# Loading K and V for two batches at a time in a decode attention kernel

## The chip, the cores and the metric

The kernel runs on one core of a Trainium2 chip. The time is that of the device, in microseconds (us), from the start to the end of one execution; the median of three runs of the kernel before is 202.74 us (202.69 to 202.88). The profile is of one further execution of 202.94 us. A core has a TensorE for matmuls (PE; its weight loads are PEld), a VectorE (DVE), a ScalarE (ACT), a GpSimd (POOL), a SyncE that issues most transfers (SP), and 16 DMA engines that move the data between device memory and the on-chip memories' 128 partitions. TensorE's results go to PSUM, everything else lies in SBUF.

## The reference

There are two branches on the same input `x` (8 batches, one token, 448 features), mixed by a sigmoid gate `g`. Branch A is attention over a cache; branch B is a layer norm and a small MLP.

```python
W = min(4096, max(256, Sk // 4))           # Sk = 4096, so W = 1024 keys
q = (x @ wq) -> [B=8, Hq=16, 1, Dh=256]
k = k_cache[:, :, Sk - W:, :]              # [8, Hkv=8, 1024, 256], each used by rep = 2 heads
v = v_cache[:, :, Sk - W:, :]
p = softmax(q k^T * Dh ** -0.5)            # over the 1024 keys
a = (p v) -> [8, 4096] @ wo                # wo: 4096 x 448
b = gelu(layernorm(x) @ w1 + b1) @ w2 + b2
return g * a + (1 - g) * b                 # all tensors bfloat16
```

Only the last 1024 of 4096 keys of each cache are read: 8 batches x 8 KV heads x 1024 keys x 256 features x 2 bytes is 32 MB for K and as much for V.

## The kernel before, in words

**Setting.** A *pair* `n` is one KV head `g` and one batch `b` (`g, b = divmod(n, 8)`), 64 pairs in all; the eight pairs of one head are a *group*. A tile of K or of V is one pair: 128 partitions with `NC = 8` keys of 256 features each, so that partition p holds the keys 8p to 8p + 7, 4 KB that are contiguous in device memory. The whole tile is 512 KB in one piece.

**Loads.** `load` (L116 to L119) takes a tile from `kvpool`, which has `NKV = 23` buffers, and issues one transfer on SP. The order of issue is the list `units` (L137 to L145): K of pair 0, 1, 2, ...; from pair 11 on a V tile after each K tile, eleven pairs behind (`NB + LAG`, 8 + 3); after each eighth K the 448 KB of `wo` that this group needs; at the end the last eleven V tiles and the last piece of `wo`. Ahead of them SP issues `x`, `w1`, `w2`, three transfers of `wq` with 8 KB per partition (L134), and the rest of `wq`, `wq_t` (L135). There are eight DMA semaphores in turn, so each transfer of SP waits for the landing of the one eight places before it; from the 24th tile on it also waits until TensorE has read the tile whose buffer it takes.

**TensorE's order.** Nothing reorders the program: the schedule is written by hand (`manual_schedule`), and each engine works through its instructions in the order of the text. First come the MLP (`mlp_up`, `mlp_down`) and the q projection. Then a loop of 75 steps `n` (L428 to L455) does, in each step,

- `transposes(n)`: 16 transposes of 128 x 128 turn the K tile round into PSUM, and two copies on VectorE bring it to SBUF as `kt` (L314, L319);
- `scores(n - 1)`: 16 matmuls with `kt` as weights and the two query heads of this batch as 2 columns (L330). The scores of a group stand in one PSUM bank `G[g]`: keys on the partitions, and 8 chunks x 16 columns (8 batches x 2 heads) beside each other;
- in the first three steps of the next group the softmax of the last one: `soft_max1` takes the maximum over chunks on VectorE, `soft_max2` a transpose and the maximum over the partitions, and splits it in three bfloat16 parts; `soft_exp` subtracts it by a matmul into the scores and applies the exponential on ScalarE (L370, L377), 128 columns in each;
- `pv(n - 11)`: 16 matmuls with the V tile as weights and 2 columns of the exponentials (L396), summing over the chunks;
- after the last `pv` of a group `soft_sum`: 8 matmuls with a matrix of ones sum the exponentials (L382), VectorE takes the reciprocal and scales (`o_scale`, L387, L407); one step later `o_proj` multiplies by `wo` into `A_ps` (L421).

After the loop the last `o_proj`, the mix with branch B (L458) and the store follow.

Of the kernel before, what the change touches and what calls it, by code (L numbers as in the profile page):

```python
# [9 lines left out]
ALU = mybir.AluOpType  # L10
AXIS = mybir.AxisListType
BF16 = mybir.dt.bfloat16
# [4 lines left out]
def kernel(  # L17
# [15 lines left out]
    nc = tc.nc  # L33
    P = nc.NUM_PARTITIONS

    B, Sq, D = A_x.shape
    _, Hkv, Sk, Dh = A_k_cache.shape
    HD = A_wq.shape[1]
    Hq = HD // Dh
    rep = Hq // Hkv  # L40
    W = min(4096, max(256, Sk // 4))
    kv0 = Sk - W
    F = B_w1.shape[1]
    NB = B
    NJ = Dh // P
    NC = W // P
    NF = F // P
    R = NB * rep
    DC = D // P
    DM = DC * P  # L50
    TL = D - DM
    HH = HD // 2
    assert Sq == 1 and Dh % P == 0 and W % P == 0 and F % P == 0
    assert TL * 2 == P and TL % 32 == 0 and NC * R <= P and 3 * 32 <= P and R <= 32
    qscale = float(Dh) ** -0.5
    NPAIR = NB * Hkv
    LAG = 3
    NKV = 23


    S0 = 0
    O0 = S0 + NC * R
    Z0 = O0 + NJ * R
    T0 = Z0 + R

# [3 lines left out]
    consts = ctx.enter_context(tc.tile_pool(name="consts", bufs=1))  # L69
    kvpool = ctx.enter_context(tc.tile_pool(name="kvpool", bufs=NKV))  # L70
    ktpool = ctx.enter_context(tc.tile_pool(name="ktpool", bufs=3))
# [15 lines left out]
    gw_sb = consts.tile([NB, D], BF16, name="gw_sb")  # L87
    wq_sb = consts.tile([P, DC, HD], BF16, name="wq_sb")
    wq_t = consts.tile([P, HH], BF16, name="wq_t")
    w1_sb = consts.tile([P, DC, F], BF16, name="w1_sb")  # L90
    w1_t = consts.tile([P, F], BF16, name="w1_t")
# [4 lines left out]
    ident = consts.tile([P, P], BF16, name="ident")  # L96
    identf = consts.tile([P, P], F32, name="identf")
    onesb = consts.tile([P, P], BF16, name="onesb")
    diag = [consts.tile([P, R], BF16, name=f"diag{k}") for k in range(2)]
    qT = consts.tile([P, NJ, Hkv, NB, rep], BF16, name="qT")  # L100
    xT = consts.tile([P, DC + 2, NB], BF16, name="xT")
    yT = consts.tile([P, DC + 1, NB], BF16, name="yT")
    x_e = consts.tile([NB, 2, P], BF16, name="x_e")
# [3 lines left out]
    res = consts.tile([NB, D], BF16, name="res")  # L107


    def k_src(src, n):  # L110
        g, b = divmod(n, NB)
        return src[b, g, kv0:Sk, :].rearrange("(p c) d -> p c d", c=NC)

    KV = {}

    def load(kind, n):  # L116
        t = kvpool.tile([P, NC, Dh], BF16, tag="kv", name="kv")
        nc.sync.dma_start(t[:], k_src(A_k_cache if kind == "K" else A_v_cache, n))  # L118
        KV[kind, n] = t  # L119

    nc.sync.dma_start(x_sb[:], xf)
# [3 lines left out]
    nc.sync.dma_start(  # L125
        w1_sb[:], B_w1[0:DM, :].rearrange("(p c) n -> p c n", c=DC)
    )
# [6 lines left out]
        nc.sync.dma_start(wq_sb[:, c, :], wq_v[:, c, :])  # L134
    nc.sync.dma_start(wq_t[:], A_wq[DM:D, :].rearrange("r (h n) -> (r h) n", h=2))  # L135

    units = []  # L137
    for n in range(NPAIR):
        units.append(("K", n))
        if n % NB == NB - 1 and n // NB < Hkv - 1:  # L140
            units.append(("W", n // NB))
        if n - NB - LAG >= 0:
            units.append(("V", n - NB - LAG))
    units += [("V", m) for m in range(NPAIR - NB - LAG, NPAIR)]
    units += [("W", Hkv - 1)]  # L145
    pos = [0, 0]

    def issue_to(k):
        while pos[0] < len(units):
            kind, n = units[pos[0]]  # L150
            if kind == "W":
                r0 = n * NKH * P
                nc.sync.dma_start(
                    wo_sb[n][:],
                    A_wo[r0 : r0 + NKH * P, :].rearrange("(k p) n -> p k n", p=P),
                )
            else:
                if pos[1] == k:
                    return
                load(kind, n)  # L160
                pos[1] += 1
            pos[0] += 1

    issue_to(NKV)


    make_identity(nc, ident[:])
    nc.gpsimd.memset(onesb[:], 1.0)
    for t in diag:
        nc.gpsimd.memset(t[:], 0.0)  # L170
    nc.gpsimd.memset(x_e[:], 0.0)
# [108 lines left out]
    for c in range(DC + 1):  # L280
        for k in range(NQ):
            if c < DC:
                w, xs = wq_sb[:, c, k * P : (k + 1) * P], xT[:, c, :]
            else:
                h, kk = divmod(k, NQ // 2)
                w, xs = wq_t[:, kk * P : (kk + 1) * P], xT[:, DC + h, :]
            nc.tensor.matmul(
                q_ps[:, k * NB : (k + 1) * NB],
                lhsT=w,
                rhs=xs,  # L290
                start=(c == 0 and k == 0),
                stop=(c == DC),
                skip_group_check=True,
# [9 lines left out]
    G = {}  # L303
    E = {}
# [1 line left out]
    RZ = {}  # L306

    def transposes(n):
        K = KV.pop(("K", n))
        kt = ktpool.tile([P, NJ, W], BF16, tag="kt", name="kt")  # L310
        for j in range(NJ):
            ktp = ps_kt.tile([P, W], BF16, tag="ktp", name="ktp")
            for c in range(NC):
                nc.tensor.transpose(  # L314
                    ktp[:, c * P : (c + 1) * P],
                    K[:, c, j * P : (j + 1) * P],
                    ident[:],
                )
            nc.vector.tensor_copy(kt[:, j, :], ktp[:])  # L319
        KT[n] = kt  # L320

    def scores(n):
        g, b = divmod(n, NB)
        kt = KT.pop(n)
        if b == 0:
            G[g] = ps_g.tile([P, 512], F32, tag="grp", name="grp")
        for c in range(NC):
            for j in range(NJ):
                s = S0 + c * R + b * rep
                nc.tensor.matmul(  # L330
                    G[g][:, s : s + rep],
                    lhsT=kt[:, j, c * P : (c + 1) * P],
                    rhs=qT[:, j, g, b, :],
                    start=(b == 0 and c == 0 and j == 0),
                    stop=(j == NJ - 1),
                    skip_group_check=True,
                )
# [42 lines left out]
    def soft_sum(g):  # L380
        for c in range(NC):
            nc.tensor.matmul(  # L382
                G[g][:, Z0 : Z0 + R], lhsT=onesb[:], rhs=E[g][:, c * R : (c + 1) * R],
                start=False, stop=(c == NC - 1), skip_group_check=True,
            )
        rz = work.tile([P, R], F32, tag="rz", name="rz")
        nc.vector.reciprocal(rz[:], G[g][:, Z0 : Z0 + R])  # L387
        RZ[g] = rz

    def pv(m):  # L390
        g, b = divmod(m, NB)
        V = KV.pop(("V", m))
        for j in range(NJ):
            for c in range(NC):
                o = O0 + j * R + b * rep
                nc.tensor.matmul(  # L396
                    G[g][:, o : o + rep],
                    lhsT=V[:, c, j * P : (j + 1) * P],
                    rhs=E[g][:, c * R + b * rep : c * R + (b + 1) * rep],
                    start=False,  # L400
                    stop=(c == NC - 1),
                    skip_group_check=True,
                )

    def o_scale(g):
        ot = work.tile([P, NJ, R], BF16, tag="ot", name="ot")
        nc.vector.tensor_tensor(  # L407
            ot[:],
            G[g][:, O0 : O0 + NJ * R].rearrange("p (j r) -> p j r", j=NJ),
            RZ[g][:].unsqueeze(1).to_broadcast([P, NJ, R]),  # L410
            op=ALU.mult,
        )
        OT[g] = ot

    def o_proj(g):
        ot = OT[g]
        for i in range(rep):
            for j in range(NJ):
                k = i * NJ + j
                w = wo_sb[g][:, k, :]  # L420
                nc.tensor.matmul(  # L421
                    A_ps[:],
                    lhsT=ot[:].rearrange("p j (b i) -> p j i b", i=rep)[:, j, i, :],
                    rhs=w,
                    start=(g == 0 and k == 0),
                    stop=(g == Hkv - 1 and k == NKH - 1),
                )


    LAST = NPAIR + NB + LAG  # L430
    done = 0
    for n in range(LAST):
        if n < NPAIR:
            transposes(n)
            done += 1
        if 0 <= n - 1 < NPAIR:
            scores(n - 1)
        g, r = divmod(n, NB)
        if g >= 1 and g - 1 < Hkv:
            if r == 0:  # L440
                soft_max1(g - 1)
            if r == 1:
                soft_max2(g - 1)
            if r == 2:
                soft_exp(g - 1)
        m = n - NB - LAG
        if m >= 0:
            pv(m)
            done += 1
            if m % NB == NB - 1:  # L450
                soft_sum(m // NB)
                o_scale(m // NB)
            if m % NB == 0 and m > 0:
                o_proj(m // NB - 1)
        issue_to(NKV + done)  # L455
    o_proj(Hkv - 1)

# [34 lines left out]
```

## Time and profile before

| what | value |
|---|---|
| median of three runs | 202.74 us (202.69 to 202.88) |
| the profiled execution | 202.94 us |
| its span | 201.2 us |
| TensorE busy (matmuls) | 161.7 us, 80% |
| VectorE busy | 106.7 us, 53% |
| transfers of SP's queue | 77.45 MB, 95.9% of 16 DMA engines' span |
| mean granted clock of TensorE | 0.79 |
| K and V transfers | 64 each, 512 KB, 9.9 us from issue to landing |

How to read it: the page divides the span in 40 slices of 5 us and gives for each the busy share of the engines, the granted clock of TensorE and the GB/s of the DMA engines. The chain that ended last goes back from the last instruction to what released it, and so on to the start; it says what the span consists of. The groups give the busy time and the mean of one instruction by line. The waits say which engine stood idle for which other, and how long. The timeline lists instructions in order of time: start, duration, engine, line, operation, how many.

### The profile page before, as it was taken

To read this page: it belongs to the slowest core of one execution; us is meant where nothing else is said; L and a number is where in the kernel's file an instruction comes from. 1 tells how busy PE (TensorE), PEld (TensorE's weight loads), DVE (VectorE), ACT (ScalarE), POOL (GpSimd) and SP (SyncE) were. 2 spreads that over 40 slices of the span, in tenths; PEclk is the share of its full clock that TensorE was granted. 3 is DMA by queue.
4 is the path that set the end of the run, shared out by engine and by line. 5 is a ranking of instruction groups with operands and counts; after the bars stand their busy time and mean duration, and the time that the engine had idled before them with its cause. 6 is when DMAs were issued, how large, how long until landed. Compare 5 with 4: busy or idle time off the path is not lost.

```text
span 201.2 us, 7399 instructions
## 1 busy us (share of the span) xinstructions
PE 161.7 (80%) x3392; PEld 146.6 (73%) x3392; DVE 106.7 (53%) x241; ACT 5.6 (3%) x13; POOL 1.4 (1%) x11
## 2 busy tenths in 40 slices
PE   0268999987899759979898789777999899785753
PEld 0162799977898759879887789677897898785440
DVE  4220189995575526755495448544673658554001
ACT  3200000000000000000000000000000000000000
POOL 2000000000000000000000000000000000000000
PEclk9999979999669856985599757988556969975555
DMA  5999999999999999999999999999999999999930
GB/s 185 343 415 414 415 416 411 414 415 406 414 419 419 404 418 420 416 407 415 420 415 411 411 420 412 416 414 413 415 425 404 412 416 421 415 415 415 371 133 1
DMA packets 23682, 78.15 MB, mean 389 GB/s; under 512 B 2314, under 2 KB 6435, under 8 KB 23012
## 3 DMA queue, kind: packets, MB, share of 16 engines
q1 hardware_dynamic: 23552, 77.45, 95.9%
q8 instruction: 26, 0.43, 0.8%
q10 hardware_dynamic: 100, 0.24, 0.4%
q14 instruction: 4, 0.03, 0.0%
HBM read 77.68 MB, written 0.01 MB: 386 GB/s over the span
## 4 chain that ended last, share of the span: by engine, by line
DMA 91%; PE 6%; DVE 1%; issue 0%; ACTq 0%; SPq 0%; DVEq 0%
DMA kv<-in_A_v_cache_dram 42%; DMA kv<-in_A_k_cache_dram 40%; DMA wq_t<-in_A_wq_dram 6%; DMA w_t<-in_B_w_dram 4%; PE ktp L314 3%; PE A_ps L421 1%; PE grp L396 1%; PE grp L330 1%; DVE res L458 0%; ACTq L122 0%; DVE rz L387 0%; PE grp L382 0%; DVE ot L407 0%; SPq L118 0%; DVEq L387 0%
## 5 line engine op out<-in xcount | busy, mean ns | idle before, releaser
L319 DVE COPY kt<-ktp 128x1024 bf16<-128x1024 bf16 x128 | 84.2, 688 | 56.5 <-PE ktp L314 56.0
L314 PE MATMUL ktp<-ident,kv 128*128 128x128 bf16 x1024 | 86.2, 252 | 12.6 <-DMA kv<-in_A_k_cache_dram 12.6
L314 PEld LDWEIGHTS <-kv 128*128 128x128 bf16 x1024 | 74.5, 115 | 18.0 <-DMA kv<-in_A_k_cache_dram 16.1
L396 PE MATMUL grp<-e,kv 128*128 128x2 bf16 x1024 | 35.9, 165 | 9.1 <-DMA kv<-in_A_v_cache_dram 7.9
L396 PEld LDWEIGHTS <-kv 128*128 128x128 bf16 x1024 | 32.1, 100 | 13.0 <-DMA kv<-in_A_v_cache_dram 10.4
L330 PE MATMUL grp<-qT,kt 128*128 128x2 bf16 x1024 | 36.3, 165 | 0.3 <-DVE kt L319 0.2
L330 PEld LDWEIGHTS <-kt 128*128 128x128 bf16 x1024 | 34.8, 100 | 0.5 <-DVE kt L319 0.3
L421 PE MATMUL A_ps<-wo_sb,ot 128*8 128x448 bf16 x32 | 9.6, 433 | 0.6 <-DVE ot L407 0.6
L387 DVE RECIPROCAL rz<-grp 128x16 f32<-128x16 f32 x8 | 2.0, 254 | 11.6 <-PE grp L382 11.6
L261 PE MATMUL b_ps<-w_sb,hT 128*8 128x448 bf16 x14 | 5.4, 573 | 2.1 <-DVE hT L255 2.1
L377 ACT ACTIVATE e<-grp 128x128 bf16<-128x128 f32 x8 | 2.2, 278 | 167.3 <-PE grp L370 167.3
L261 PEld LDWEIGHTS <-hT 128*8 128x8 bf16 x14 | 1.6, 122 | 5.2 <-issue 2.9
L421 PEld LDWEIGHTS <-ot 128*8 128x8 bf16 x32 | 2.4, 93 | 3.4 <-issue 1.5
L211 PE MATMUL tp<-ident,y_sb 8*128 8x8 bf16 (+1 forms) x4 | 0.4, 181 | 5.5 <-DVE y_sb L193 5.5
L237 PE MATMUL h_ps<-yT,w_t 65*128 65x8 bf16 x14 | 2.8, 201 | 2.4 <-DMA w_t<-in_B_b_dram 2.4
L211 PEld LDWEIGHTS <-y_sb 8*128 8x128 bf16 (+1 forms) x4 | 0.3, 110 | 5.5 <-DVE y_sb L193 5.5
L237 PE MATMUL h_ps<-yT,w_sb 128*128 128x8 bf16 x42 | 3.5, 202 | 0.7 <-DMA w_sb<-in_B_w_dram 0.7
L237 PEld LDWEIGHTS <-w_sb 128*128 128x128 bf16 x42 | 3.4, 159 | 0.8 <-DMA w_sb<-in_B_w_dram 0.8
L237 PEld LDWEIGHTS <-w_t 65*128 65x128 bf16 x14 | 2.2, 158 | 2.4 <-DMA w_t<-in_B_w_dram 2.4
L249 DVE COPY z<-h_ps 128x112 f32<-128x112 f32 x1 | 0.3, 275 | 6.6 <-PE h_ps L237 6.6
L272 DVE TENSOR_SCALAR bvec<-b_ps,omg_sb 8x448 f32<-8x448 f32 x1 | 0.7, 672 | 5.7 <-PE b_ps L268 5.7
L370 PE MATMUL grp<-diag,onesb 128*128 128x128 bf16 x8 | 1.8, 229 | 2.3 <-DVE diag L364 2.0
(61 smaller groups left out, 44.6 us busy)
## 6 DMA issues: line engine op xcount, KB each, us to landing
kv<-in_A_k_cache_dram SPq DMA_DIRECT2D x64, 512.0 KB, 9.9
kv<-in_A_v_cache_dram SPq DMA_DIRECT2D x64, 512.0 KB, 9.9
wo_sb<-in_A_wo_dram SPq DMA_DIRECT2D x8, 448.0 KB, 9.9
wq_sb<-in_A_wq_dram SPq DMA_DIRECT2D x3, 1024.0 KB, 12.7
w_sb<-in_B_w_dram SPq DMA_DIRECT2D x1, 1568.0 KB, 10.7
w_sb<-in_B_w_dram SPq DMA_DIRECT2D x1, 1344.0 KB
wq_t<-in_A_wq_dram SPq DMA_DIRECT2D x1, 512.0 KB, 11.1
w_t<-in_B_w_dram ACTq DMA_DIRECT2D x1, 224.0 KB, 8.5
```

The source lines that it names most:

```text
L211: nc.tensor.transpose(tp[0:w, c * NB : (c + 1) * NB], s, ident[0:NB, 0:NB])
L237: nc.tensor.matmul(o, lhsT=w.rearrange("p (q k) -> p k q", k=NF)[:, k, :], rhs=yT[0:kp, c, :], start=(c == 0), stop=(c == DC),)
L261: nc.tensor.matmul(b_ps[0:NB, 0:D], lhsT=M["hT"][:, k * NB : (k + 1) * NB], rhs=w2_sb[:, k, :], start=(k == 0), stop=False,)
L272: nc.vector.tensor_scalar_mul(bvec[:], b_ps[0:NB, 0:D], omg_sb[:])
L314: nc.tensor.transpose(ktp[:, c * P : (c + 1) * P], K[:, c, j * P : (j + 1) * P], ident[:],)
L319: nc.vector.tensor_copy(kt[:, j, :], ktp[:])
L330: nc.tensor.matmul(G[g][:, s : s + rep], lhsT=kt[:, j, c * P : (c + 1) * P], rhs=qT[:, j, g, b, :], start=(b == 0 and c == 0 and j == 0), ...
L370: nc.tensor.matmul(G[g][:, S0 : S0 + NC * R].rearrange("p (c r) -> p c r", c=NC), lhsT=onesb[:], rhs=diag[g % 2][:].unsqueeze(1).to_broadc ...
L377: nc.scalar.activation(e[:], G[g][:, S0 : S0 + NC * R], ACT.Exp)
L387: nc.vector.reciprocal(rz[:], G[g][:, Z0 : Z0 + R])
L396: nc.tensor.matmul(G[g][:, o : o + rep], lhsT=V[:, c, j * P : (j + 1) * P], rhs=E[g][:, c * R + b * rep : c * R + (b + 1) * rep], start=False,
L421: nc.tensor.matmul(A_ps[:], lhsT=ot[:].rearrange("p j (b i) -> p j i b", i=rep)[:, j, i, :], rhs=w, start=(g == 0 and k == 0), stop=(g == ...
```

## The change

A tile of K or V now holds two neighbouring batches (`TB = 2`) of one head, a *unit*; there are 32 units of 1 MB, and 12 buffers in place of 23. Partition p holds 16 keys (`NC = 16`), 8 KB that are contiguous in device memory, of batch `p % 2` of the two: even partitions hold the first batch and odd ones the second. The steps of the loop stay 64 + 11; each step takes one half of a unit, that is 8 of its 16 chunks (`HC = 8`), from both batches. The last V unit is loaded in two halves.

Since a chunk of 128 keys now has keys of both batches, it is multiplied with the queries of both (4 columns in place of 2), and the half where key and query are of different batches must not count. So a matmul at the start of each group writes the bank: `par` (which batch a partition is of) times `cross` (0 for the same batch, -1e30 for the other), 256 columns. The scores add to that. The exponentials of the masked half are zero, so `pv` can sum over all partitions. The scores of a group are 16 x 16 = 256 columns now, and so are the maximum, the exponential, and the number of sums in `soft_sum` (16 in place of 8), whose code does not change.

```diff
+    TB = 2
+    NC = W * TB // P
+    HC = NC // TB
...
+    RU = TB * rep
+    NBU = NB // TB
...
-    NKV = 23
+    NKV = 12
+    NEG = -1.0e30
...
     def load(kind, n):
         t = kvpool.tile([P, NC, Dh], BF16, tag="kv", name="kv")
-        nc.sync.dma_start(t[:], k_src(A_k_cache if kind == "K" else A_v_cache, n))
+        src = A_k_cache if kind == "K" else A_v_cache
+        g, u = divmod(n, NBU)
+        parts = TB if (kind, n) == ("V", NU - 1) else 1
+        w = NC // parts
+        for q in range(parts):
+            nc.sync.dma_start(
+                t[:, q * w : (q + 1) * w, :].rearrange("p c d -> p (c d)"),
+                src[u * TB : (u + 1) * TB, g, kv0:Sk, :].rearrange(
+                    "t (r c) d -> r t c d", c=NC
+                )[:, :, q * w : (q + 1) * w, :].rearrange("r t c d -> r t (c d)"),
+            )
         KV[kind, n] = t
...
+    VU = (SPG + LAG) // TB
     units = []
-    for n in range(NPAIR):
+    for n in range(NU):
         units.append(("K", n))
...
+    nc.vector.memset(cross[:], 0.0)
+    nc.gpsimd.affine_select(
+        out=cross[:], in_=cross[:], compare_op=ALU.is_equal, fill=NEG, base=0,
+        pattern=[[-1, TB], [0, rep]], channel_multiplier=1,
+    )
+    nc.vector.memset(par[:], 1.0)
+    nc.gpsimd.affine_select(
+        out=par[:].rearrange("t (r u) -> t r u", u=TB),
...
     def transposes(n):
-        K = KV.pop(("K", n))
+        u, h = divmod(n, TB)
+        K = KV["K", u]
...
-                    K[:, c, j * P : (j + 1) * P],
+                    K[:, h * HC + c, j * P : (j + 1) * P],
...
     def scores(n):
...
             G[g] = ps_g.tile([P, 512], F32, tag="grp", name="grp")
-        for c in range(NC):
+            nc.tensor.matmul(
+                G[g][:, S0 : S0 + NC * R].rearrange("p (c r) -> p c r", r=RU),
+                lhsT=par[:],
+                rhs=cross[:].rearrange("t u i -> t (u i)").unsqueeze(1).to_broadcast(
+                    [TB, NC * NBU, RU]
+                ),
+                start=True, stop=True, skip_group_check=True,
+            )
+        for c in range(HC):
             for j in range(NJ):
-                s = S0 + c * R + b * rep
+                s = S0 + (h * HC + c) * R + bu * RU
                 nc.tensor.matmul(
-                    G[g][:, s : s + rep],
+                    G[g][:, s : s + RU],
                     lhsT=kt[:, j, c * P : (c + 1) * P],
-                    rhs=qT[:, j, g, b, :],
-                    start=(b == 0 and c == 0 and j == 0),
+                    rhs=qT[:, j, g, bu * TB : (bu + 1) * TB, :].rearrange(
+                        "p t i -> p (t i)"
+                    ),
+                    start=False,
...
     def pv(m):
...
-            for c in range(NC):
-                o = O0 + j * R + b * rep
+            for c in range(HC):
+                cc = h * HC + c
+                o = O0 + j * R + bu * RU
                 nc.tensor.matmul(
-                    G[g][:, o : o + rep],
-                    lhsT=V[:, c, j * P : (j + 1) * P],
-                    rhs=E[g][:, c * R + b * rep : c * R + (b + 1) * rep],
+                    G[g][:, o : o + RU],
+                    lhsT=V[:, cc, j * P : (j + 1) * P],
+                    rhs=E[g][:, cc * R + bu * RU : cc * R + (bu + 1) * RU],
```

More of the change, by code (lines that the diff above doesn't have):

```diff
@@ L45 @@
     NJ = Dh // P
-    NC = W // P
+    TB = 2
+    NC = W * TB // P
+    HC = NC // TB
     NF = F // P
     R = NB * rep
+    RU = TB * rep
+    NBU = NB // TB
     DC = D // P
@@ L53 @@
     assert Sq == 1 and Dh % P == 0 and W % P == 0 and F % P == 0
-    assert TL * 2 == P and TL % 32 == 0 and NC * R <= P and 3 * 32 <= P and R <= 32
+    assert TL * 2 == P and TL % 32 == 0 and NC * R <= 2 * P and NB % TB == 0 and 3 * 32 <= P and R <= 32
     qscale = float(Dh) ** -0.5
-    NPAIR = NB * Hkv
+    NU = NBU * Hkv
+    NSTEP = NU * TB
+    SPG = NBU * TB
     LAG = 3
-    NKV = 23
+    NKV = 12
+    NEG = -1.0e30
     S0 = 0
@@ L98 @@
     onesb = consts.tile([P, P], BF16, name="onesb")
+    par = consts.tile([TB, P], BF16, name="par")
+    cross = consts.tile([TB, TB, rep], BF16, name="cross")
     diag = [consts.tile([P, R], BF16, name=f"diag{k}") for k in range(2)]
@@ L107 @@
     res = consts.tile([NB, D], BF16, name="res")
-    def k_src(src, n):
-        g, b = divmod(n, NB)
-        return src[b, g, kv0:Sk, :].rearrange("(p c) d -> p c d", c=NC)
     KV = {}
@@ L135 @@
     nc.sync.dma_start(wq_t[:], A_wq[DM:D, :].rearrange("r (h n) -> (r h) n", h=2))
+    VU = (SPG + LAG) // TB
     units = []
-    for n in range(NPAIR):
+    for n in range(NU):
         units.append(("K", n))
[L140 to L144, printed above, removed]
+        if n % NBU == NBU - 1 and n // NBU < Hkv - 1:
+            units.append(("W", n // NBU))
+        if n - VU >= 0:
+            units.append(("V", n - VU))
+    units += [("V", m) for m in range(NU - VU, NU)]
     units += [("W", Hkv - 1)]
@@ L168 @@
     nc.gpsimd.memset(onesb[:], 1.0)
+    nc.vector.memset(cross[:], 0.0)
[6 more added lines that the diff above has]
+        out=par[:].rearrange("t (r u) -> t r u", u=TB),
+        in_=par[:].rearrange("t (r u) -> t r u", u=TB),
+        compare_op=ALU.is_equal, fill=0.0, base=0,
+        pattern=[[0, P // TB], [-1, TB]], channel_multiplier=1,
+    )
     for t in diag:
@@ L308, in transposes @@
     def transposes(n):
-        K = KV.pop(("K", n))
+        u, h = divmod(n, TB)
+        K = KV["K", u]
+        if h == TB - 1:
+            del KV["K", u]
         kt = ktpool.tile([P, NJ, W], BF16, tag="kt", name="kt")
@@ L322, in scores @@
     def scores(n):
-        g, b = divmod(n, NB)
+        u, h = divmod(n, TB)
+        g, bu = divmod(u, NBU)
         kt = KT.pop(n)
-        if b == 0:
+        if bu == 0 and h == 0:
             G[g] = ps_g.tile([P, 512], F32, tag="grp", name="grp")
-        for c in range(NC):
+            nc.tensor.matmul(
[5 more added lines that the diff above has]
+                start=True, stop=True, skip_group_check=True,
+            )
+        for c in range(HC):
             for j in range(NJ):
-                s = S0 + c * R + b * rep
+                s = S0 + (h * HC + c) * R + bu * RU
                 nc.tensor.matmul(
-                    G[g][:, s : s + rep],
+                    G[g][:, s : s + RU],
                     lhsT=kt[:, j, c * P : (c + 1) * P],
-                    rhs=qT[:, j, g, b, :],
-                    start=(b == 0 and c == 0 and j == 0),
+                    rhs=qT[:, j, g, bu * TB : (bu + 1) * TB, :].rearrange(
+                        "p t i -> p (t i)"
+                    ),
+                    start=False,
                     stop=(j == NJ - 1),
@@ L390, in pv @@
     def pv(m):
-        g, b = divmod(m, NB)
-        V = KV.pop(("V", m))
+        u, h = divmod(m, TB)
+        g, bu = divmod(u, NBU)
+        V = KV["V", u]
+        if h == TB - 1:
+            del KV["V", u]
         for j in range(NJ):
-            for c in range(NC):
-                o = O0 + j * R + b * rep
+            for c in range(HC):
+                cc = h * HC + c
+                o = O0 + j * R + bu * RU
                 nc.tensor.matmul(
-                    G[g][:, o : o + rep],
-                    lhsT=V[:, c, j * P : (j + 1) * P],
-                    rhs=E[g][:, c * R + b * rep : c * R + (b + 1) * rep],
+                    G[g][:, o : o + RU],
+                    lhsT=V[:, cc, j * P : (j + 1) * P],
+                    rhs=E[g][:, cc * R + bu * RU : cc * R + (bu + 1) * RU],
                     start=False,
-                    stop=(c == NC - 1),
+                    stop=(cc == NC - 1),
                     skip_group_check=True,
@@ L427, in o_proj @@
                 )
-    LAST = NPAIR + NB + LAG
+    LAST = NSTEP + SPG + LAG
     done = 0
     for n in range(LAST):
-        if n < NPAIR:
+        if n < NSTEP:
             transposes(n)
-            done += 1
-        if 0 <= n - 1 < NPAIR:
+            done += n % TB == TB - 1
+        if 0 <= n - 1 < NSTEP:
             scores(n - 1)
-        g, r = divmod(n, NB)
+        g, r = divmod(n, SPG)
         if g >= 1 and g - 1 < Hkv:
@@ L445 @@
                 soft_exp(g - 1)
-        m = n - NB - LAG
+        m = n - SPG - LAG
         if m >= 0:
             pv(m)
[L449 to L454, printed above, removed]
+            done += m % TB == TB - 1
+            if m % SPG == SPG - 1:
+                soft_sum(m // SPG)
+                o_scale(m // SPG)
+            if m % SPG == 0 and m > 0:
+                o_proj(m // SPG - 1)
         issue_to(NKV + done)
```

## The prediction

> **What bounds the kernel now.** I read the page's first three parts first, to see which resource has no slack, then the chain that ended last, then what the engines wait for, and last single stretches of the timeline for the pace of the loads and of one step of TensorE.
>
> ```profile
> span 201.2 us, 7399 instructions
> PE 161.7 (80%) x3392; PEld 146.6 (73%) x3392; DVE 106.7 (53%) x241; ACT 5.6 (3%) x13; POOL 1.4 (1%) x11
> GB/s 185 343 415 414 415 416 411 414 415 406 414 419 419 404 418 420 416 407 415 420 415 411 411 420 412 416 414 413 415 425 404 412 416 421 415 415 415 371 133 1
> q1 hardware_dynamic: 23552, 77.45, 95.9%
> q8 instruction: 26, 0.43, 0.8%
> DMA 91%; PE 6%; DVE 1%; issue 0%; ACTq 0%; SPq 0%; DVEq 0%
> ```
>
> The DMA queue is full from 10 us to 186 us at about 415 GB/s, and 91% of the chain is transfers. TensorE at 80% is second. So a change here is worth what it does to the pace of the loads and to what follows the last load; TensorE matters only if it stops keeping up.
>
> The pace of the loads can be read from SP, because each load waits for the landing of the one eight places earlier:
>
> ```profile
> 12.30 0.33 SPq L118 DMA_DIRECT2D kv<-in_A_k_cache_dram  x1
> 14.79 0.33 SPq L118 DMA_DIRECT2D kv<-in_A_k_cache_dram  x1
> 17.27 0.33 SPq L118 DMA_DIRECT2D kv<-in_A_k_cache_dram  x1
> 19.77 0.33 SPq L118 DMA_DIRECT2D kv<-in_A_k_cache_dram  x1
> ...
> 42.34 0.43 SPq L118 DMA_DIRECT2D kv<-in_A_k_cache_dram  x1
> ...
> 59.83 0.33 SPq L118 DMA_DIRECT2D kv<-in_A_k_cache_dram  x1
> ```
>
> The first issue is released by the landing of w2, the other three by the landings of the three wq loads. Those are 1 MB each with 8 KB per partition, the shape that K and V are to get: (19.77 - 12.30) / 3 = 2.49 us for 1 MB. Between 42.34 and 59.83 SP issues 14 loads of 512 KB with 4 KB per partition: 1.249 us each, 2.498 us for 1 MB.
>
> Then TensorE, one step at half the clock and one at the full clock, and its waits:
>
> ```profile
> 145.17 1.87 PE L314 MATMUL ktp<-ident,kv 128*128 128x128 bf16 x16
> 148.05 1.87 PE L314 MATMUL ktp<-ident,kv 128*128 128x128 bf16 x16
> ...
> 156.51 1.05 PE L314 MATMUL ktp<-ident,kv 128*128 128x128 bf16 x16
> 158.21 1.05 PE L314 MATMUL ktp<-ident,kv 128*128 128x128 bf16 x16
> ...
> PE ktp L314 <- DMA kv<-in_A_k_cache_dram: 12.6, 23, 0.7
> PE grp L396 <- DMA kv<-in_A_v_cache_dram: 7.9, 11, 1.7
> ```
>
> A step is 1.70 us at clock 1.0 and 2.88 us at 0.5 (that one holds an exp and a sum), against 2.498 us for its K and its V. TensorE waits for loads for 20.5 us in all: that is the cover for added work.
>
> **The change part by part.**
>
> *Loads.* 128 loads of 512 KB become 63 of 1 MB and two halves; per DMA engine 1024 packets of 4 KB become 496 of 8 KB and 32 of 4 KB. Bytes are the same. Taken from the wq loads, 64 MB at 2.49 instead of 2.498 us: **-0.5 us**. Bounds: the trace's packet records give 159.9 ns for 4 KB and 313.8 ns for 8 KB; 512 x (319.8 - 313.8) = 3.1 us, and 63 semaphore packets fewer at 9 ns are 0.6 us, so at most -3.7 us. I don't take that, since packets overlap (the busy share of the engines is 1.03 in the stretches) and the spacing of landings is what counts. From the other side, the seven K loads that land right after wq_t come 1.225 us apart in the landing records, 2.45 us for 1 MB, which is faster than wq's 8 KB rows: by that pair 8 KB costs 64 x 0.04 = +2.6 us. The value from wq against the steady stretch stands between and compares the same shape with the same length of run.
>
> [...]
>
> *SP.* 63 issues of 0.33 us fall away; SP waits on landings anyway. 0.
>
> *Pool.* 23 buffers of 512 KB become 12 of 1 MB. Eight loads are in flight by the lane waits, so four buffers (10 us of loading) hold what has landed and is in use. K needs about two steps, 3.4 to 5.8 us; V is freed a step after the next K landed, 2.5 + 3 us. SP will sometimes wait for TensorE, but with five or more loads in flight the queue doesn't run dry. 0, as long as TensorE lags by less than some 5 us.
>
> *Head.* The first K lands 1.25 us later, about 25.0 us; TensorE is at the q matmuls until 24.8 us. The two memsets on VectorE (85 ns each by the yT row) stand ahead of work that waits 1.6 us for gw_sb. The two selects on POOL (293 ns by the ident row) delay diag, x_e and identf, which are wanted from 15 us on. 0.
>
> *Scores and PV.* The number of matmuls stays; they get 4 columns instead of 2. Rows with 2 and with 8 columns show 165 and 166 ns. 0.
>
> *Added on TensorE, per group of eight batches:* a mask matmul of 256 columns, an exp matmul of 256 instead of 128, 16 sums instead of 8. By L421 (448 columns, 0.92 us for four at full clock, 1.65 at half) a column is 0.5 or 0.9 ns: 0.12/0.23 and 0.06/0.11 us; eight sums are 0.20/0.29 us by the timeline. That is 0.38 us at full and 0.63 at half clock, some 4 us over eight groups, within the 20.5 us of waits. 0 on the path but for the last group:
>
> *End.* pv of the last half load, sums, reciprocal, scaling and projection follow the last landing at 194.88 us. The eight sums run there from 195.37 at half clock; eight more are **+0.3 us**. The longer max and exp of the last group (283 and 278 ns rows, about 0.1 us more each) come earlier. The last K now brings steps 62 and 63 together, so one half-clock step more (2.6 us) comes after it: exp moves from 184.3 to about 187.3. Eight pv at 0.5 and a projection of 1.65 us then end the backlog near 193.1, before the last halves land at 193.6 and 194.9. Hidden with half a microsecond to spare; lost, it costs up to 1 us.
>
> *Instructions.* TensorE gets 144 more on 6778. One packet of q8 is 16 KB and about 1 us of an engine (0.8% of 16 x 201.2 us over 26); four links of the chain last 11.4 to 11.6 us instead of 9.9, which I read as such a packet on the slowest engine. One packet more on that engine: +1.5 us at most; I take 0, because only four of the 26 show in the chain.
>
> **Sum.** The profiled execution took 202.94 us (span 201.2 and 1.7 around it), 0.2 above the median. 202.94 - 0.5 + 0.3 = 202.74; less 0.2, **202.5 us** as a median.
>
> **The rivals.**
>
> *Fewer packets do pay.* For: the wo loads (448 KB in runs of 896 B, 32 packets per engine) come 1.21 us apart in the landing records, where 448/512 of 1.249 is 1.09; the 0.12 us over 24 more packets is 5 ns each, and 512 fewer give 2.6 us. Against: wq. Time: 202.7 - 2.6 + 0.3 = 200.4 us.
>
> *TensorE becomes the bound (slower).* The granted clock, averaged over 52 to 182 us in stretches of 10, is 0.76, half speed 48% of the time. A group costs 14.9 us at full and 23.0 at half clock, with the added work 15.3 and 23.6; per step 1.91 + 1.04 x share = 2.41 us at 48%. It passes 2.498 us at a share of 56%, a mean clock of 0.72. For: only 3% of room, and the clock falls by itself. Against: backlogs of the half-clock stretches are caught up in each full one. At a mean clock of 0.70, 2.54 us: 52 steps x 0.04 = 2 us, 204.7 us; at 0.68, 206.7 us.
>
> *Two streams 16 MB apart are slower than one.* Neighbouring partitions now read from two batches, 8 x 4096 x 512 B = 16 MB apart. Against: the engines are spread over several loads by the end (the slices 371 and 133 are engines that finish early), so rows of different batches were read at once, and SP's pace stays at 1.25 us. For: the fast K stretch above was the one with the engines closest together, 2% faster than later. Another 2% would be 3.2 us: 205.7 us.
>
> [...]
>
> *The end loses its cover*, as above: 203.5 us.
>
> **How the numbers follow.** Forecast (pace of the wq loads, 201.8 to 202.9) 0.35; fewer packets pay 0.30; TensorE 0.12; two streams 0.13; the end, or an instruction packet more, 0.10. Faster by over 0.2% (0.4 us, about what a measurement of this kernel can tell) is the second case and a part of the first: 0.38; within 0.2%: 0.28; slower: 0.34. The range leaves out a tenth on either side: down to 200.0, a little past the packet case, and up to 205.5, past TensorE at 0.70; the forecast's own range is 201.8 to 203.1.
>
> **What would show it.** In the changed kernel SP should issue a 1 MB load every 2.49 us; 2.45 would be the packet case, 2.54 the two streams. The waits of TensorE for K and V should shrink from 20.5 to about 16 us; near zero, with SP waiting for grp or ktp, would be the TensorE case. From the last V's landing to the end of res it was 3.9 us (194.88 to 198.74); I expect 4.2, and 4.7 or more would mean that the end lost its cover. The prediction is wrong if 8 KB runs move more than 422 GB/s, or if the granted clock falls below 0.72.

## The result

The changed kernel takes 203.13 us (median of 19 runs, 202.75 to 203.33) against 202.69 us for the kernel before in the same sessions (19 runs): a ratio of 1.0018, 95% interval 1.0011 to 1.0025. It is 0.4 us slower, a small but clear loss, where the forecast was 0.2 us less than before. The profiled execution took 203.13 us, its span 201.4 us.

First the page of the changed kernel, the parts shown of the kernel before:

```profile
span 201.4 us, 7433 instructions
PE 169.6 (84%) x3464; PEld 149.6 (74%) x3464; DVE 109.5 (54%) x243; ACT 6.4 (3%) x13; POOL 2.2 (1%) x13
GB/s 201 335 422 412 421 408 417 418 412 405 421 415 417 408 420 415 417 411 420 413 420 413 412 417 413 416 412 414 417 418 408 420 417 417 415 418 409 337 120 1
q1 hardware_dynamic: 14480, 77.45, 94.4%
q8 instruction: 27, 0.44, 0.9%
DMA 81%; PE 14%; SPq 2%; issue 1%; DVE 1%; DVEq 0%
```

The packets of SP's queue fell from 23552 to 14480, and the GB/s stayed where they were. SP's timeline gives the pace of the 1 MB loads:

```profile
38.73 1.84 SPq L129 DMA_DIRECT2D kv<-in_A_v_cache_dram  x1
41.21 1.84 SPq L129 DMA_DIRECT2D kv<-in_A_k_cache_dram  x1
43.69 1.54 SPq L129 DMA_DIRECT2D kv<-in_A_v_cache_dram  x1
46.19 0.54 SPq L129 DMA_DIRECT2D kv<-in_A_k_cache_dram  x1
48.71 0.54 SPq L129 DMA_DIRECT2D kv<-in_A_v_cache_dram  x1
```

(48.71 - 38.73) / 4 = 2.495 us for 1 MB: almost the wq pace of 2.49, and about as much as the 2.498 us before. So by these rows half the packets bought nothing. The last V landed at 194.97 us in this execution, at 194.88 in that of before. The rest is the end. Its chain, first before, then after (start, duration, what):

```profile
194.92 0.59 PE grp L396 x16
195.51 0.24 PE grp L382 x8
```

```profile
195.01 0.59 PE grp L445 x16
195.60 0.45 PE grp L427 x16
```

The sixteen sums take 0.2 us more than the eight. The waits (who for whom, us in all, times, longest) show the two things that the forecast had to call harmless:

```profile
PE ktp L347 <- DMA kv<-in_A_k_cache_dram: 8.4, 9, 1.9
PE grp L445 <- DMA kv<-in_A_v_cache_dram: 2.6, 4, 1.5
...
SPq L129 <- PE ktp L347: 35.3, 27, 3.1
```

TensorE's waits for loads fell from 20.5 to 11 us, and SP now waits for TensorE to free buffers, up to 3.1 us at a time. Whether either cost something had to be tried, and above all why 8 KB runs did not pay.

### The profile page after: what moved, and what is told of

Its sections match the earlier page's. It is cut to its first block, busy times and chain, and to the rows that moved or that the text cites. A ratio compares the mean times of both kernels' runs of the same rounds, so it can differ in the third digit from the quotient of the medians.

```text
span 201.4 us, 7433 instructions
## 1 busy us (share of the span) xinstructions
PE 169.6 (84%) x3464; PEld 149.6 (74%) x3464; DVE 109.5 (54%) x243; ACT 6.4 (3%) x13; POOL 2.2 (1%) x13
## 3 DMA queue, kind: packets, MB, share of 16 engines
q1 hardware_dynamic: 14480, 77.45, 94.4%
## 4 chain that ended last, share of the span: by engine, by line
DMA 81%; PE 14%; SPq 2%; issue 1%; DVE 1%; DVEq 0%
DMA kv<-in_A_k_cache_dram 47%; DMA kv<-in_A_v_cache_dram 19%; DMA wo_sb<-in_A_wo_dram 9%; PE ktp L347 7%; DMA wq_sb<-in_A_wq_dram 6%; PE grp L373 2%; PE grp L445 2%; PE A_ps L470 2%; SPq L129 1%; PE grp L427 0%; DVE res L507 0%; PE grp L362 0%; SPq L146 0%; SPq L137 0%; PE grp L394 0%
## 5 line engine op out<-in xcount | busy, mean ns | idle before, releaser
L347 PE MATMUL ktp<-ident,kv 128*128 128x128 bf16 x1024 | 87.5, 253 | 9.8 <-DMA kv<-in_A_k_cache_dram 8.4
L347 PEld LDWEIGHTS <-kv 128*128 128x128 bf16 x1024 | 75.3, 115 | 15.6 <-DMA kv<-in_A_k_cache_dram 9.5
L445 PE MATMUL grp<-e,kv 128*128 128x4 bf16 x1024 | 35.9, 166 | 3.4 <-DMA kv<-in_A_v_cache_dram 2.6
L373 PE MATMUL grp<-qT,kt 128*128 128x4 bf16 x1024 | 36.8, 166 | 1.3 <-issue 1.0
L445 PEld LDWEIGHTS <-kv 128*128 128x128 bf16 x1024 | 32.6, 100 | 6.9 <-DMA kv<-in_A_v_cache_dram 3.1
L470 PE MATMUL A_ps<-wo_sb,ot 128*8 128x448 bf16 x32 | 12.7, 549 | 0.6 <-DVE ot L456 0.6
L422 ACT ACTIVATE e<-grp 128x256 bf16<-128x256 f32 x8 | 3.1, 383 | 168.3 <-PE grp L415 168.3
L427 PE MATMUL grp<-e,onesb 128*128 128x16 bf16 x128 | 4.6, 174 | 0.0
L415 PE MATMUL grp<-diag,onesb 128*128 128x256 bf16 x8 | 2.9, 361 | 1.8 <-DVE diag L409 1.8
L427 PEld LDWEIGHTS <-onesb 128*128 128x128 bf16 x128 | 4.0, 104 | 0.0
L386 DVE TENSOR_REDUCE pm<-grp 128x16 f32<-128x256 f32 x8 | 3.3, 418 | 1.1 <-PE grp L373 1.1
```

Source lines behind the costliest of these rows:

```text
L347: nc.tensor.transpose(ktp[:, c * P : (c + 1) * P], K[:, h * HC + c, j * P : (j + 1) * P], ident[:],)
L373: nc.tensor.matmul(G[g][:, s : s + RU], lhsT=kt[:, j, c * P : (c + 1) * P], rhs=qT[:, j, g, bu * TB : (bu + 1) * TB, :].rearrange("p t i - ...
L386: nc.vector.reduce_max(pm[:], G[g][:, S0 : S0 + NC * R].rearrange("p (c r) -> p r c", r=R), axis=AXIS.X,)
L415: nc.tensor.matmul(G[g][:, S0 : S0 + NC * R].rearrange("p (c r) -> p c r", c=NC), lhsT=onesb[:], rhs=diag[g % 2][:].unsqueeze(1).to_broadc ...
L422: nc.scalar.activation(e[:], G[g][:, S0 : S0 + NC * R], ACT.Exp)
L427: nc.tensor.matmul(G[g][:, Z0 : Z0 + R], lhsT=onesb[:], rhs=E[g][:, c * R : (c + 1) * R], start=False, stop=(c == NC - 1), skip_group_chec ...
```

## The experiments

The first theory was that bytes alone set the pace, so runs of 4 and 8 KB are alike, and that the loss is the longer end. The rival was that fewer packets do pay and something else in the changed kernel eats the gain.

**Runs of 4 KB in the changed kernel.**

```diff
-        parts = TB if (kind, n) == ("V", NU - 1) else 1
+        parts = TB
```

> Every unit of the changed kernel is loaded by two transfers of 512 KB with runs of 4 KB, as only the last V unit was; compute, order and layout are those of the changed kernel. If the pace of the loads is set by bytes, 64 MB take the same 2.495 us per MB and the time stays within 0.3 us of the changed kernel's 203.1 us. If fewer and longer packets do pay but something else in the changed kernel eats the gain, this kernel loses it: 2.6 us by the 5 ns per packet of the wo loads, about 205.7 us.

Measured: 207.29 us (ratio to before 1.0218, interval 1.0205 to 1.0231), 4.2 us more than the changed kernel. The first theory falls: halving the runs, which also doubles the number of transfers, costs more than any bound from the trace had allowed, 8 ns for each of some 500 packets. But then something else costs as much in the changed kernel, since its 4 KB version is 4.6 us slower than the kernel before, which has 4 KB runs as well.

**The longer end alone,** in the kernel before:

```diff
     def soft_sum(g):
+        if g == Hkv - 1:
+            for c in range(NC):
+                nc.tensor.matmul(
+                    G[g][:, X0 : X0 + R], lhsT=onesb[:], rhs=E[g][:, c * R : (c + 1) * R],
...
         for c in range(NC):
```

> The kernel before, with eight more sums of the exponentials in the last group alone, ahead of the eight that count and into columns that nobody reads. If the longer end explains what the change cost, this costs 0.25 to 0.3 us, 202.95 us against 202.69; if the end is hidden by the last piece of wo or by the reciprocal, it costs nothing.

Measured: 203.01 us against 202.72 (ratio 1.001, interval 1.0 to 1.0021). The 0.3 us for the sums agree in size; the interval just reaches zero.

**Sums and reciprocals off the end,** in the changed kernel and in the kernel before:

```diff
             pv(m)
+            if m % SPG == 0:
+                soft_sum(m // SPG)
...
-                soft_sum(m // SPG)
                 o_scale(m // SPG)
```

> The changed kernel with the sums and the reciprocal of each group moved from after its last PV to after its first one, so that 16 sums (0.45 us) and the reciprocal (0.3 us with its wait) leave the end. If everything after the last landing counts fully: 0.8 us less than the changed kernel, 202.3 us. If another wait takes over at the end (the last piece of wo lands 1.1 us after the last V), 0.4 us or less.

> The same move in the kernel before, where 8 sums (0.3 us) and the reciprocal leave the end: 0.6 us less than before if the end counts fully, 202.1 us. The difference to the changed kernel with the same move is what the change costs without the sums: 0.1 to 0.2 us if the loads are no faster, -0.5 us if the pace of the wq loads holds for K and V.

Measured: 202.62 us for the changed kernel, 0.5 us less than without the move; 202.38 us for the kernel before (ratio 0.9986, interval 0.9977 to 0.9995), 0.3 us less. Both fall short of the full gain; the first lies between its two cases (0.8 us, and 0.4 or less). The end of the chain of the changed kernel with early sums:

```profile
178.61 17.67 DMA wo_sb<-in_A_wo_dram
...
196.32 1.67 PE A_ps L470 x4
```

The projection now waits for the last piece of `wo`, which is loaded behind the last V. With the move the two still differ by 0.2 us, so nothing here shows the loads of the changed kernel to be faster.

**Loads alone.** All transfers in their order, no compute; four lengths of run:

```diff
+    issue_to(10 ** 6)
+    nc.vector.tensor_copy(bvec[:, 0:1], KV["V", NPAIR - 1][0:NB, NC - 1, Dh - 1 : Dh])
+    nc.vector.tensor_copy(res[:], wo_sb[Hkv - 1][0:NB, 0, :])
+    nc.sync.dma_start(out_f, res[:])
-    make_identity(nc, ident[:])
...
```

> Loads alone: all transfers of the kernel before in their order, with no matmul, softmax or MLP; one value of the last V and one row of the last wo are read at the end and stored, so the output is not the reference's. K and V are loaded in runs of 2 KB here (two transfers of 256 KB per tile). If bytes set the pace, within 1 us of the loads with 4 KB runs; if each packet costs 5 ns, 1024 more per DMA engine cost 5 us.

> Loads alone, with the 4 KB runs of the kernel before. TensorE's program is gone, so the instruction packets should go too; if these delay single DMA engines by 1.5 us each and the slowest sets the end, the last V lands about 6 us earlier than the 194.9 us of the full kernel, near 189 us. If they don't matter, it lands at 194 to 195 us.

> Loads alone, with the units of the changed kernel: 8 KB runs from two batches. Bytes set the pace: within 0.5 us of the 4 KB runs. Packets pay: 2.6 us less. Two streams 16 MB apart cost: more than the 4 KB runs by 1 us or more.

> Loads alone, with four batches per unit: 16 KB runs, 2 MB transfers, six buffers. Bytes set the pace: within 0.5 us of 8 KB. Packets pay: 1.3 us less than 8 KB. Streams cost: more than 8 KB.

Measured: 209.81, 199.12, 194.50 and 191.82 us. Longer runs pay at every step, without any compute: 10.7, 4.6 and 2.7 us for 1024, 504 and 240 packets of data less per DMA engine, 9 to 11 ns a packet. Each step also about halves the number of transfers. The 4-byte packet that comes once per transfer and engine takes 9 ns in the packet records (the start, duration and size of every packet in the trace; 9.06 ns on average for the 2288 of SP's queue in the kernel before), so between 4 and 8 KB 63 x 9 ns = 0.6 us of the 4.6 can be theirs, an estimate; the length of the run and the size of the transfer were not tried apart.

The 4 KB loads, though, did not behave as in the full kernel. By the landing records (when each DMA engine reported its part of a transfer as landed) they came 1.28 us apart, or 1.276 with the smaller `wo` transfers averaged in; in the kernel before, with all its compute beside them, the same transfers come 1.249 us apart, or 1.246. Taking work away had made them slower, so something in the transfers themselves had changed. In the programs it is the address. The K and V buffers begin in each partition at byte 112896 in the kernel before, which is 441 x 256. In the changed kernel the new tiles `par` and `cross` (288 bytes) stand ahead of them and they begin at 113184, 32 bytes past a multiple of 256; in the loads alone, where other tiles are missing, 160 bytes (2 and 4 KB) and 192 bytes (8 and 16 KB) past one.

**The address, from both sides.** One constant tile that nobody reads puts the buffers back in the changed kernel, or shifts them in the kernel before. It also moves the compute tiles that lie behind it, `kt` and the exponentials among them; the loads alone, further down, have none of these.

```diff
     cross = consts.tile([TB, TB, rep], BF16, name="cross")
+    pad = consts.tile([P, 112], BF16, name="pad")
```

```diff
     onesb = consts.tile([P, P], BF16, name="onesb")
+    pad = consts.tile([P, 16], BF16, name="pad")
```

> The changed kernel with one more constant tile of 224 bytes that nobody reads, so that the K and V buffers begin at a multiple of 256 bytes in their partition, as they do in the kernel before (address 112896); in the changed kernel the tiles par and cross moved them to 113184, 32 bytes past one. If that offset costs each packet some 3.5 ns (1.247 us per 512 KB in the kernel before against 1.275 us with 4 KB runs at an offset), 512 packets per DMA engine give 1.8 us: 201.3 us. If the address doesn't matter: 203.1 us.

> The kernel before with one more constant tile of 32 bytes that nobody reads, so that its K and V buffers begin 32 bytes past a multiple of 256. If the offset costs 3.5 ns per packet, 1024 packets per DMA engine cost 3.6 us: 206.3 us, and the loads come 1.275 us apart. If the address doesn't matter: 202.7 us.

> The changed kernel with every unit loaded in two transfers of 4 KB runs (207.3 us before the move), its buffers moved back to a multiple of 256. If the address is all that made it slow: 1.247 us per 512 KB and 203.3 us, which leaves nothing for the two streams. If reading two batches at a time costs too: between 204 and 207 us.

Measured: the changed kernel with its buffers at a multiple of 256 takes **200.34 us** (ratio to before 0.989, interval 0.9871 to 0.9909). The kernel before with a shift of 32 bytes takes 206.98 us (1.0208, 1.0192 to 1.0224). The changed kernel with 4 KB runs and aligned buffers takes 203.33 us (1.0028, 1.0018 to 1.0039). SP's timeline of the changed kernel with aligned buffers, and of the kernel before with the shift:

```profile
36.60 1.87 SPq L130 DMA_DIRECT2D kv<-in_A_k_cache_dram  x1
39.09 1.52 SPq L130 DMA_DIRECT2D kv<-in_A_v_cache_dram  x1
...
48.88 0.54 SPq L130 DMA_DIRECT2D kv<-in_A_v_cache_dram  x1
```

```profile
53.26 0.33 SPq L119 DMA_DIRECT2D kv<-in_A_k_cache_dram  x1
...
60.93 0.59 SPq L119 DMA_DIRECT2D kv<-in_A_k_cache_dram  x1
```

(48.88 - 36.60) / 5 = 2.456 us for 1 MB instead of 2.495, and (60.93 - 53.26) / 6 = 1.278 us for 512 KB instead of 1.249. A tile that is never touched moves the pace of every K and V load. Put together, in us:

| | buffers at a multiple of 256 | 32 bytes past it |
|---|---|---|
| kernel before, 4 KB runs | 202.7 | 207.0 |
| two batches, 4 KB runs | 203.3 | 207.3 |
| two batches, 8 KB runs | 200.3 | 203.1 |

The change went from the upper left to the lower right. Across, the offset costs 4.0 to 4.3 us with 1024 packets and 2.8 us with 520, that is 4 to 5.4 ns a packet. Down, the longer runs, with half as many transfers, are worth 3.0 us aligned and 4.2 us at the offset.

The packet records show the same one packet at a time. A packet of 4 KB takes 159.9 ns on average in the kernel before and 163.4 ns with the shift; one of 8 KB takes 310.9 ns in the changed kernel with aligned buffers and 315.7 ns without the tile. Eight packets of 8 KB are one engine's part of 1 MB, and 8 x 4.8 = 38 ns is the distance from 2.456 to 2.495 us. So by these means the offset costs time within the packets, not between the transfers.

**Both improvements together.** The first `diff` of the two above and the move of the sums.

> Buffers at a multiple of 256 and the sums and reciprocals off the end, together. If both effects hold and add, 201.3 - 0.5 = 200.8 us or a little less, which is below both kernels; if the address does nothing, 202.6 us as with the sums alone.

Measured: **199.75 us** (ratio to before 0.9854, interval 0.984 to 0.9868), 3 us below the kernel before and below the expectation, which had put the gain from the address at 1.8 us; it was 2.8.

**Where wq lies, and the transfers alone.** `wq` is at 128 bytes past a multiple of 256 in every kernel here.

```diff
+    pad = consts.tile([P, 48], BF16, name="pad")
```

> The changed kernel with its K and V buffers moved to 128 bytes past a multiple of 256, which is also where wq lies in every kernel here. If only a multiple of 256 is fast, 203.1 us as at 32 bytes; if 128 is enough, 200.4 us.

> Loads alone in 4 KB runs (output not the reference's, as before), with the buffers at a multiple of 256; they lay 160 bytes past one in the first run of loads alone (199.1 us). If the address acts in the transfers and not through TensorE or VectorE, 1.247 us per 512 KB and about 195.2 us. The last V should then land near 189.5 us, against 194.9 in the kernel before: the difference is what the instruction packets cost there.

> Loads alone in 8 KB runs (output not the reference's), buffers at a multiple of 256 instead of 192 bytes past one (194.5 us): 2.455 us per MB as in the full kernel with aligned buffers, and 192.1 us. If loads alone are bound by something else, 194.5 us.

Measured: the changed kernel at an offset of 128 takes 202.25 us (0.9974, 0.9962 to 0.9985), between the aligned 200.34 and the 203.13 at 32 bytes, and its landings are 2.48 to 2.49 us apart, as wq's were. Its 8 KB packets take 314.4 ns. So not every offset costs the same, but 128 bytes take away two thirds of what the address gives. The loads alone with aligned buffers (two runs of each) take 194.73 us with 4 KB runs (199.12 at an offset of 160) and 192.11 us with 8 KB runs (194.50 at 192): with no TensorE and no PSUM in the program, and two small copies on VectorE at its end, differences of 4.4 and 2.4 us remain. The stretches of the loads alone with 4 KB runs (span, us; engines; PEclk; DMA share; GB/s), first at the offset, then aligned:

```profile
60.00:80.00 20.00, 0.00 (x0) 0.00 (x0) 1.00 1.03 408
110.00:130.00 20.00, 0.00 (x0) 0.00 (x0) 1.00 1.03 408
```

```profile
60.00:80.00 20.00, 0.00 (x0) 0.00 (x0) 1.00 1.03 417
110.00:130.00 20.00, 0.00 (x0) 0.00 (x0) 1.00 1.03 419
```

The DMA share reads 1.03 in both: a full queue looks the same, whether it moves 408 or 419 GB/s. The mean of a 4 KB packet tells them apart, 163.3 ns at the offset and 159.0 aligned.

## Why the prediction was wrong

*The step that failed is the price of the loads,* "Taken from the wq loads, 64 MB at 2.49 instead of 2.498 us: -0.5 us". The pace was right, 2.495 us, and the reason for it was wrong. The pair compared two things at once: the wq loads have 8 KB runs at an offset of 128 bytes, the steady K and V loads 4 KB runs at a multiple of 256. The two differences nearly cancel, and I read the remainder as the price of the run. K and V in 8 KB runs, put at 128 bytes themselves, do come at wq's pace, 2.48 to 2.49 us. The one fact that decides, where the buffers lie, was not in the sum at all: the two small tiles `par` and `cross` were costed only by the instructions that fill them, not by what they push along. In the place of -0.5 the runs showed -3.0 for the longer runs with half as many transfers and +2.8 for the offset (on the 8 KB runs), -0.2 together.

*Fewer packets do pay* was the rival that had the mechanism, given 0.30. With aligned buffers the changed kernel shows the sign that the prediction named for it, a load every 2.456 us (2.45), and takes 200.34 us where the rival had 200.4. Its 5 ns a packet is close to what the aligned loads alone show, (194.73 - 192.11) / 504 = 5.2 ns, and its 2.6 us stands against 3.0 us in the full kernel.

That the 5 ns came out of the wo loads is in part luck, because they were not a clean pair either. A wo tile begins at a multiple of 256, but its rows are 896 bytes apart, so every second one begins 128 bytes past such a multiple, while the K and V loads beside it did not. If those 16 rows per engine cost 3.5 ns more each, as 8 KB packets do at 128 bytes (314.4 against 310.9), that is 0.06 of the 0.12 us, an estimate. The packet records, set aside because packets overlap, were mixed in the same way: the 313.8 ns were wq's, at 128 bytes. With 310.9 ns the same sum gives 504 x 8.9 ns = 4.5 us instead of 3.1, more than the 3.0 us that the time showed.

The cost did not grow with the offset: on the 8 KB runs 32 bytes past a multiple of 256 cost 2.8 us (203.13 against 200.34) and 128 bytes 1.9 us (202.25 against 200.34). What moved is the place written to; the places read from are the same. How the address acts inside the transfer stays open: the runs show the time of the packets and no more.

*The end* was right: +0.3 expected, 0.3 from the sums alone, 0.2 in the profile. The backlog after the last K was gone by 191 us, with 1.5 us of waiting left (the forecast had 0.5), so its cover held.

*The look-ahead* was right in its price, wrong in its size: SP waits for TensorE for 35 us in all, but the loads alone, with no buffer waiting for TensorE, keep the same pace (in the landing records 2.487 us for 1 MB at 192 bytes against 2.493 in the full kernel at 32, and 2.45 us in both when aligned). *TensorE as the bound* did not come, though the margin shrank more than forecast: busy time grew by 8 us instead of 4 (the mean clock was 0.76 instead of 0.79), and its waits fell to 11 us, not 16. *Two streams* cost nothing in the loads: the 4 KB loads from two batches come 1.247 us apart when aligned, as those from one. What remains of the 0.5 us between the kernel before and its two-batch form with aligned 4 KB runs is 0.3 us of sums and 0.2 us that were not settled. Not settled either is the stretch of K loads behind wq_t that the prediction took as its upper bound: 1.225 us apart, at the same address as the later ones at 1.249.

*Instructions:* 27 packets in place of 26; in the landing records the slowest DMA engine falls back four times in either kernel, so the price of 0 held. Two counts of the prediction are off without weight: the new loads are 504 packets of 8 KB and 16 of 4 KB per engine, not 496 and 32, and TensorE has 2 x 3392 = 6784 rows, not 6778.

## What to carry to other kernels

Before a row of the trace is used as the price of a transfer, look at what else differs between the two transfers; the byte at which the buffer begins in its partition belongs to it, and it is in the program, not in the profile. Here two new constant tiles, 288 bytes together, moved every buffer that is allocated behind them by 288, and the 32 bytes past a multiple of 256 that came of it cost 2.8 us. In a kernel bound by its loads, put the large buffers first, or let them begin at a multiple of 256 bytes, which was the fastest start tried here (200.34 us, against 202.25 at 128 bytes past one and 203.13 at 32). When a change shows no effect at all where one was argued, try its opposite in place (here the short runs): two effects that cancel look the same as none.

## What the runs showed of the hardware

- The start of a buffer within its partition changed the pace of loads from 2.456 to 2.495 us per MB with 8 KB runs and from 1.249 to 1.278 us per 512 KB with 4 KB runs. Both are for an offset of 32 bytes. An offset of 128 bytes gave 2.48 to 2.49 us per MB; in the loads alone 192 bytes gave 2.487 us per MB (2.45 aligned) and 160 bytes 1.28 us per 512 KB (1.249 in the kernel before, aligned). Each of the four was slower than a multiple of 256.
- In loads alone each packet more cost 5 ns when aligned (4 against 8 KB runs, 194.73 against 192.11 us) and 9 to 11 ns at an offset (2 to 16 KB runs, 209.81 to 191.82 us), the greater number of transfers included.
- With loads alone and the same pace as in the kernel before (4 KB, aligned), the last V is there 5.3 us earlier. The group that reads it (idle time behind the bar, and what ended it):

```profile
L168 DVE CAST bvec<-kv 8x1 f32<-8x1 bf16 x1 | 0.1, 142 | 189.6 <-DMA kv<-in_A_v_cache_dram 189.6
```

In the landing records of the kernel before, the slowest DMA engine falls back four times by about 1.5 us, each time at one of the 26 instruction packets (at every eighth of them, from the first at 21.0 us), and lies 6.3 us behind the fastest at the last V; in the loads alone, where TensorE has no program, there are no such packets, and the spread is 1.3 us. That these packets are the whole of the 5.3 us was not tried by itself.
